# Another stated order of five engines, and a stated place for every ring tile, in a one-core attention and two-MLP kernel

## The chip, the cores and the metric

One of the cores of a Trainium2 chip runs the whole program. Five engines work side by side: TensorE (PE in the rows, with its weight loads as PEld), VectorE (DVE), ScalarE (ACT), GpSimd (POOL) and SyncE (SP), which issues all the DMAs here. The metric is the device time of one execution in microseconds; the time before is the median of 3 runs.

## The reference, cut to what matters

Causal attention with a memory term, then two MLPs, all over 2304 tokens (4 batches of 576) in float32:

```python
scores = scale * q @ k.T                       # B=4, H=8, S=576, D=64, causal
a = softmax(scores); local = a @ v
q_p = where(q > 0, q, exp(q) - 1) + 1
mem_out = (q_p @ M_prev) / (q_p . z_prev + 1e-6)
x = g * mem_out + (1 - g) * local              # g = sigmoid(beta) of each head; x is 2304 x 512
h = x @ w_in;  r = max(h, 0)                   # 512 -> 2048
x = (s * r * r + b) @ w_out                    # 2048 -> 512
h = x @ w2_in                                  # 512 -> 1024
solu = h * softmax(h)
ln = (solu - mean) / sqrt(var + 1e-6) * g_ln
out = ln @ w2_out                              # 1024 -> 512
```

## The kernel before

**Stages.** Three stages overlap at their edges. The first (to about 270 us) is the attention: 16 units (a unit u is two heads of one batch), each in five steps. `scores` multiplies K and Q (L592, and L623 for the last 64 rows), VectorE subtracts the maximum (L608, L626), ScalarE takes the exponential (L575), TensorE transposes (L649), ScalarE copies out of PSUM (L653), `values` multiplies by V (L681) and `memory` adds the memory term (L693, L697, L699). Into the gaps go the weights' decoding (L370 to L406) and the first quarter of the first MLP (`first_part`, L712 to L779). The second stage (270 to 545 us) is the rest of the first MLP: `hidden` (L712 to L720) and `ystep` (L927 to L929), over five blocks of up to 512 tokens, twice. The third (545 to 800 us) is the second MLP, nine pairs q of token tiles t = 2q and 2q + 1: `products` (42 wide matmuls, L1001 to L1004, by a scheme with seven products), `front` (softmax and layer norm), `back` (8 transpositions L1050, 24 wide matmuls L1059 to L1061, the copy L1063, the output's DMA L1064). A float32r matmul is done in three (high by high, high by low, low by high).

**Two paths that the prediction follows.** From unit 4 on, the reciprocals of a unit are turned over (L522, `turn`), copied (L524), written to DRAM (L526, tile rd) and read back, spread over the partitions (L529, tile RW, two DMAs); GpSimd multiplies phi(q) by them (L547, `weigh_q`, tile mq), and TensorE can then do L697 and L699. In the third stage the last product of a token tile is reduced on VectorE (L1007), exponentiated (L1029, ScalarE), scaled (L1030 to L1032, VectorE), squared (L1036, ScalarE), brought to a variance (L1037, VectorE), to the power -0.5 (L1038, GpSimd) and normed (L1039, VectorE); then L1050 transposes it.

**What sets the order.** The program is traced in the order of the Python code; `ORDER` then lists for every engine the numbers of its traced instructions (`606` is the 607th matmul, `71+2` stands for 71 and 72), and `state_order` chains each to the one before it, so each engine runs its list in order and waits at the first whose operands aren't there. `SLOTS` says for some rings which buffer each successive tile takes; `Slots.tile` turns the place into a tag of its own. Numbers used below: PE 606 is L522 of unit 6, 666 and 667 are its L697; PE 3656 to 3661 are the last product of token tile 10, 3774 to 3781 its transpositions; PE 4058 to 4081 and 4090 to 4113 are the output matmuls of tiles 16 and 17; SP 70 is rd of unit 6, 71 and 72 its RW, 77 a load of M_prev, 80 and 86 stores of y, 87 a load of q; SP 88 is the store of batch 1's x (tile xd, 1152 KB), 100 is rd of unit 9, 101 and 102 its RW; SP 247 to 250 are the outputs of tiles 14 to 17.

Of the kernel before, what the change touches and what calls it, by code (L numbers as in the profile page):

```python
# [17 lines left out]
P = 128  # L18
# [182 lines left out]
    "pr3": "01010101010101010101010101010101",  # L201
    "sm": "0123401234012340",
    "mq": "0101010101010101",
    "gs.r": "010101010100101010101010100",
    "gs.g": "01234012340123401234012340",
    "ys.y": "01011010010010101011",
    "ps_h.h": "010101010101010",
# [31 lines left out]
def attention_mlp_kernel(  # L239
# [74 lines left out]
    FP1 = 4  # L314
# [818 lines left out]
```

## Time and profile before

| | |
|---|---|
| median of 3 runs | 803.94 us (803.6 to 804.2) |
| the profiled execution, span | 803.9 us, 13224 instructions |
| PE busy | 794.3 us (99%), 4866 matmul records |
| PEld busy | 645.3 us (80%) |
| DVE busy | 531.6 us (66%) |
| ACT busy | 542.5 us (67%) |
| POOL busy | 107.6 us (13%) |
| DMA | 83.55 MB, mean 104 GB/s |

The ends of matmuls are modelled, so the busy time of PE says when it had work in hand and not that it ran at its peak; its pace is read from the distance between the starts of successive matmuls. The granted clock is a share of full speed: 1.00 is the upper of TensorE's two levels (2.4 GHz), 0.50 the lower (1.2 GHz).

### The profile page before, as it was taken

What the parts mean: (1) busy time and instruction counts of PE and PEld (TensorE: products, weight loads), DVE (VectorE), ACT (ScalarE), POOL (GpSimd) and SP (SyncE); (2) the same over time, 40 slices, a digit from 0 to 9 for tenths busy, and PEclk for the clock granted to TensorE, in tenths of its full rate; (3) what the DMA queues carried; (4) which work ended last, traced back from release to release, by engine and by line L of the source; (5) the groups of instructions that cost most, each with busy time, mean ns of one, the idle gap of its engine ahead of it and who ended that gap; (6) DMA issues with size and microseconds to landing.
All of it is one profiled execution on the core that took longest, in us unless ns stands there. A gap on an engine that the chain in (4) does not pass through costs nothing.

```text
span 803.9 us, 13224 instructions
## 1 busy us (share of the span) xinstructions
PE 794.3 (99%) x4866; PEld 645.3 (80%) x4866; DVE 531.6 (66%) x1329; ACT 542.5 (67%) x1122; POOL 107.6 (13%) x126
## 2 busy tenths in 40 slices
PE   9999999999999999999999999999999999999998
PEld 6677776778777788888898888889888888888886
DVE  6999988978575465245755643465788566566662
ACT  7999988888787467666677567666765455444442
POOL 3121223211010000000000020010212222222000
PEclk9999999999999999999999999999999999999999
DMA  8563666555352426424333230021210000000001
GB/s 260 185 174 112 209 211 192 187 165 155 100 170 81 160 80 220 148 78 131 131 106 131 91 119 1 28 87 70 79 53 1 26 27 27 1 27 32 22 14 66
DMA packets 42005, 83.55 MB, mean 104 GB/s; under 512 B 6652, under 2 KB 17108, under 8 KB 41940
## 3 DMA queue, kind: packets, MB, share of 16 engines
q1 hardware_dynamic: 41940, 82.71, 31.6%
q8 instruction: 38, 0.62, 0.3%
q14 instruction: 27, 0.22, 0.1%
HBM read 68.43 MB, written 14.27 MB: 103 GB/s over the span
## 4 chain that ended last, share of the span: by engine, by line
PE 81%; ACT 2%; DVE 1%; issue 0%; POOL 0%; POOLq 0%; DVEq 0%; ACTq 0%
PE h L712 8%; PE h L713 8%; PE h L714 8%; PE y L929 6%; PE y L928 6%; PE y L927 6%; PE o L1061 4%; PE o L1060 4%; PE o L1059 4%; PE pp L649 3%; PE s L592 3%; PE po L681 2%; PE zt L1050 2%; PE y L774 2%; PE y L775 2%; PE y L776 2%
## 5 line engine op out<-in xcount | busy, mean ns | idle before, releaser
L712 PE MATMUL h<-xh,w 128*128 128x512 f32 (+1 forms) x320 | 118.7, 376 | 0.3 <-ACT r L715 0.3
L713 PE MATMUL h<-xl,w 128*128 128x512 f32 (+1 forms) x320 | 117.4, 371 | 0.0
L714 PE MATMUL h<-xh,w 128*128 128x512 f32 (+1 forms) x320 | 117.2, 371 | 0.0
L715 ACT ACTIVATE r<-h 128x512 f32<-128x512 f32 (+1 forms) x80 | 43.8, 550 | 88.3 <-PE h L714 81.7
L928 PE MATMUL y<-g,w 128*128 128x512 f32 (+1 forms) x240 | 85.4, 368 | 0.0
L929 PE MATMUL y<-g,w 128*128 128x512 f32 (+1 forms) x240 | 82.5, 368 | 0.0
L927 PE MATMUL y<-g,w 128*128 128x512 f32 (+1 forms) x240 | 81.9, 368 | 0.0
L720 DVE TENSOR_TENSOR g<-r,g 128x512 fp32r<-128x512 f32 (+1 forms) x60 | 39.1, 654 | 58.7 <-ACT r L719 58.6
L653 ACT ACTIVATE pt<-pp,omg 128x256 f32<-128x256 f32 (+3 forms) x128 | 62.4, 521 | 16.5 <-PE pp L649 12.7
L575 ACT ACTIVATE pr<-pr,mx 128x512 f32<-128x512 f32 (+3 forms) x128 | 70.7, 554 | 2.5 <-DVE mx L608 2.4
L712 PEld LDWEIGHTS h<-xh,w 128*128 128x128 f32 x320 | 60.1, 188 | 12.1 <-ACT r L715 1.3
L713 PEld LDWEIGHTS h<-xl,w 128*128 128x128 f32 x320 | 60.2, 188 | 10.2 <-DVE xl L742 0.3
L714 PEld LDWEIGHTS h<-xh,w 128*128 128x128 f32 x320 | 60.1, 188 | 10.1
L608 DVE CUSTOM_DVE_ANT_0 pr<-s,big 128x128 f32<-128x128 f32 (+3 forms) x128 | 58.4, 481 | 10.5 <-PE s L592 10.1
L1060 PE MATMUL o<-w,zh 128*128 128x512 f32 x144 | 56.9, 395 | 0.0
L1061 PE MATMUL o<-w,zl 128*128 128x512 f32 x144 | 56.5, 393 | 0.0
L1059 PE MATMUL o<-w,zh 128*128 128x512 f32 x144 | 56.3, 394 | 0.0
L649 PE MATMUL pp<-ident,pr 128*128 128x128 f32 x320 | 51.3, 283 | 0.3 <-DVE ph L481 0.2
L928 PEld LDWEIGHTS y<-g,w 128*128 128x128 f32 x240 | 44.8, 188 | 7.6
L929 PEld LDWEIGHTS y<-g,w 128*128 128x128 f32 x240 | 44.6, 188 | 7.6
L927 PEld LDWEIGHTS y<-g,w 128*128 128x128 f32 x240 | 44.6, 188 | 7.4
L649 PEld LDWEIGHTS pp<-ident,pr 128*128 128x128 f32 x320 | 36.9, 142 | 15.4 <-issue 2.8
(177 smaller groups left out, 1841.9 us busy)
## 6 DMA issues: line engine op xcount, KB each, us to landing
raw<-in_moe_w_in_dram SPq DMA_DIRECT2D x24, 512.0 KB, 6.0
raw<-in_moe_w_out_dram SPq DMA_DIRECT2D x24, 512.0 KB, 3.2
kq<-in_kq_dram SPq DMA_DIRECT2D x16, 608.0 KB, 4.9
xr<-xd SPq DMA_DIRECT2D x8, 1024.0 KB, 6.9
RW<-rd SPq DMA_DIRECT2D x24, 288.0 KB, 3.9
q<-in_q_dram SPq DMA_DIRECT2D x16, 320.0 KB, 4.2
v<-in_v_dram SPq DMA_DIRECT2D x16, 320.0 KB, 3.3
xd<-xb SPq DMA_DIRECT2D x4, 1152.0 KB
```

What stands on the lines that cost most here:

```text
L575: mark[0] = nc.scalar.activation(pr, pr, AF.Exp, bias=mx, scale=-1.0, accum_out=sm).ins
L649: nc.tensor.transpose(pp[:, e * n + c * P:e * n + (c + 1) * P], pr[:, c * P:(c + 1) * P], ident)
L653: nc.scalar.activation(p["pt", i // 2][:, j, 0:i + 1, i % 2, :], pp[:, e * n:(e + 1) * n].rearrange("p (c t) -> p c t", t=P), AF.Copy, sca ...
L712: nc.tensor.matmul(ps, wc[0], xh[:, c, 0:n], start=(c == 0), stop=False)
L713: nc.tensor.matmul(ps, wc[0], xl[:, c, 0:n], start=False, stop=False)
L714: nc.tensor.matmul(ps, wc[1], xh[:, c, 0:n], start=False, stop=(c == NC - 1))
L927: nc.tensor.matmul(o, wc[0], gh[:, 0:n], start=(f == fs[0]), stop=False)
L928: nc.tensor.matmul(o, wc[1], gh[:, 0:n], start=False, stop=False)
L929: nc.tensor.matmul(o, wc[0], gl[:, 0:n], start=False, stop=(f == fs[-1]))
L1059: nc.tensor.matmul(oo, zh, w[:, 0], start=(f == 0), stop=False)
L1060: nc.tensor.matmul(oo, zh, w[:, 1], start=False, stop=False)
L1061: nc.tensor.matmul(oo, zl, w[:, 0], start=False, stop=(f == NF2 - 1))
```

## The change

Nothing that is computed changes, and no instruction is added or removed. The five lists of `ORDER` are replaced: of 4114 matmuls 3699 stand at another place (by 13 places on average), of 941 ScalarE instructions 801, of 1115 VectorE instructions 991, of 205 DMAs 154; GpSimd's list also names four set-up instructions that had been left free. The list of TensorE is in smaller pieces: 2371 breaks between runs of successive numbers, 1325 before. Every ring of tiles gets stated places (`dec`, `wpA`, `wpB`, `gs`, `ps_h`, `tiny2`, `zq` and others had none, or only for their first tiles), and `Slots` makes each buffer of a ring a tag of one buffer. The rd tile in DRAM becomes two tiles in turn. The new order was searched for with VectorE's instructions of two operands and GpSimd's products taken to exclude one another.

```diff
 ORDER = {
     "PE": """
...
-545+2 555+4 592+6 636+6 515+12 559+2 574+2 721 576 722+6 577+3 561+10 644+8 598+8 728+5 606+2 571 608+3 681 611
-766+12 682 642+2 652+4 689+4 733+6 693+2 612+12 656+12 683+6 741+8 695+4 668 699+5 826+4 704+4 778 708+10 786+6
...
-3603 3627+2 3604+7 3629+2 3638+4 3611+3 3588+6 3614+12 3642+2 3637 3631 3646+2 3668 3672+4 3669+3 3648+8 3738 3662+6
-3656+6 3676+8 3739 3700+5 3684+8 3740+2 3705+2 3692+2 3732+6 3694 3707 3695 3742+2 3696 3708 3697+2 3750 3709+18
-3744+2 3699 3774 3727+5 3775+3 3746 3778+2 3747+3 3751+5 3782 3756+4 3780+2 3760+5 3806 3765+3 3783+5 3810+2 3768
...
-4022 3974+2 4023+3 3972+2 3976+4 4021 3981+5 4004+14 4026+19 4050+8 4045+5 4058+12 4082+2 4086+4 4070+4 4084+2
-4074+8 4090+24
...
+602+3 724 598+2 605 600+2 725+7 607 732 608 606 609 681 610+2 766+3 571 769+2 652+3 642 771+4 643 682 655 775+2
+689+4 733+4 693+2 612+10 656+8 622+2 664+4 683+3 777 686+3 737+2 741+8 695+5 826 668 700 703 701+2 827 778 828
+704+13 786+6 749 739+2 750+3 779 717+4 753+10 780 829 781+2 818+4 838+8 822+2 830 783+3 831+4 792+4 765 763+2 796
...
+3662 3705+2 3677 3656 3707 3655 3614 3657+4 3738 3661 3663+2 3615 3678 3616 3739 3617+2 3665 3732 3679 3619 3733
+3680 3620+3 3681 3666+2 3623+3 3682 3740 3683+4 3744 3687+3 3774+2 3690 3776 3741 3708 3777 3691 3778+3 3709 3781
...
+4027 4056 4011+2 4057 4013 4028 4014+3 4029 4017 4030+7 4082 4037 4083 4038+2 4084+2 4040+3 4086+2 4043 4088 4058
+4089 4044 4059 4045 4060+4 4046 4064 4047+2 4065 4049 4066+5 4090+5 4071+3 4095 4074 4096 4075 4097+3 4076 4100+3
+4077 4103+3 4078+2 4106+2 4080+2 4108+6
...
     "SP": """
-17+2 20+2 32 19 24 33 25 27 31 37 22+2 26 30 46 41+2 36 49 35 34 54 45 40 39 38 28 60 29 44 43 47 65 48 50 53 69 55
-58 52 56+2 79 51 61 66 62 73 75 74 76 63+2 85 95 68 59 70 87 80 77 72 71 96 67 81 98 82 90 83+2 86 78 111 103 91+2
-110 112 94 93 88 159 121 99+2 89 109 102 101 129 163 105+2 97 116 107+2 104 114+2 117 124 119 118 125+2 165 113
-127+2 131 122 132 123 134 133 130 120 135+2 139 138 137 140 142 141 144 143 145 158 157 160 169 161+2 164 166 179
-168 167 180 170 177 181 183+2 176 185 178 186 182 187+7 195+8 194 203+2 206+3 205 210 212 209 211 213+7 234 233 236
-235 238 237 240 239 241+5 247 246 249 248 250
+17+2 20 28 45 21 19 32 25 37 23+2 22 26 33 31 36 41+2 46 35 30 49 34 39 54 38 40 60 43 27 48 47 44 65 50 53 55 58
+56+2 79 66 69 61 52 62 76 64 63 85 68 75 74 73 67 59 77 95 70 87 72 71 80 98 81 96 82 86 84 90 29 83 159 78 111 103
+91 51 89 92 110 94 93 99 121 97 100 88 101+2 116 129 105 109 106 104 108 107 114 120 112+2 117 115 118+2 123 122 163
+124 126 125 127+2 130 132 131 134 133 136 135 137+3 143 140 142 141 144 165 157+2 145 160+3 179 177 164 169 166+3
+180+3 184 170 176 185 178 190 187+2 186 189 191 183 192 196 193 195 197+2 194 200 199 201+4 207 206 205 210 208+2
+212+2 211 214+6 234 233 235+6 242 241 244 243 245+2 248+2 247 250
 """,
 }
...
+    "dec.raw": "012012012012102102101201201201201201021021021021021021021021021021",
+    "dec.wa": "012341032410324102340132403241023401213040231402341043201340231043201340213042103401",
...
 class Slots:
-    def __init__(self, pool, name=""):
-        self.pool, self.name, self.turn = pool, name, {}
-
-    def tile(self, shape, dtype, tag=None, **k):
-        places = SLOTS.get(f"{self.name}{tag}")
-        if places:
+    def __init__(self, pool, name="", bufs=1):
+        self.pool, self.name, self.bufs, self.turn = pool, name, bufs, {}
+
+    def tile(self, shape, dtype, tag=None, bufs=None, **k):
+        bufs = bufs or self.bufs
+        if tag is None:
+            return self.pool.tile(shape, dtype, bufs=bufs, **k)
+        if bufs > 1:
+            places = SLOTS.get(f"{self.name}{tag}", "")
             n = self.turn[tag] = self.turn.get(tag, -1) + 1
-            k["bufs"] = 1
-            tag += "_" + (places[n] if n < len(places) else str(n % (int(max(places)) + 1)))
-        return self.pool.tile(shape, dtype, **({"tag": tag} if tag else {}), **k)
+            tag += "_" + (places[n] if n < len(places) else "0123456789abcdef"[n % bufs])
+        return self.pool.tile(shape, dtype, tag=tag, bufs=1, **k)
 
...
-            rd = dram.tile([2, NRW, P], F32, tag="rd", name=f"rd{u}", bufs=2)
+            rd = dram.tile([2, NRW, P], F32, tag=f"rd{u % 2}", name=f"rd{u}", bufs=1)
```

## Rows read from the trace of the kernel before

In a timeline a row has the start, the duration, the engine, the line, the operation, the tiles, how many instructions the row joins, and in brackets the idle time before it with what ended it.

**Rows 1.** Stretches: length, busy time of PE, PEld, DVE, ACT, POOL, granted clock, DMA, GB/s.

```profile
24.00:120.00 96.00, 95.11 (x852) 73.34 (x854) 92.11 (x293) 91.06 (x229) 21.00 (x19) 1.00 0.56 176
130.00:250.00 120.00, 119.88 (x1028) 92.85 (x1028) 95.02 (x298) 100.80 (x256) 20.64 (x20) 1.00 0.51 156
545.00:800.00 255.00, 254.94 (x1242) 210.94 (x1240) 165.20 (x361) 131.74 (x237) 43.25 (x55) 1.00 0.08 30
```

**Rows 2.** Timeline of PE: the turning and the memory product of unit 6.

```profile
112.28 0.30 PE L522 MATMUL tr<-ident,rw 128*128 128x128 f32 x1 [0.35 <-DVE rw L515]
...
124.75 0.43 PE L697 MATMUL pe<-mq,Mb 128*64 128x64 f32 x4 [1.88 <-POOL sums L600]
```

**Rows 3.** The stretch right after that wait, columns as in rows 1.

```profile
124.75:128.25 3.50, 3.50 (x25) 3.05 (x26) 2.76 (x14) 2.03 (x6) 0.00 (x0) 0.51 0.50 197
```

**Rows 4.** Timeline of SP: the issues between unit 6's rd and RW.

```profile
115.08 0.37 SPq L779 DMA_DIRECT2D yd<-yo  x1
116.24 1.25 SPq L529 DMA_DIRECT2D RW<-rd  x2
```

**Rows 5.** Timeline of POOL: unit 6's product.

```profile
122.94 1.76 POOL L547 TENSOR_TENSOR mq<-mq,RW 128x640 f32<-128x640 f32 x1 [4.05 <-PE pe L693]
```

**Rows 6.** Timelines of PE, SP and POOL: the same path of unit 7.

```profile
130.25 0.27 PE L522 MATMUL tr<-ident,rw 128*128 128x128 f32 x1
...
132.13 1.09 SPq L529 DMA_DIRECT2D RW<-rd  x2
...
137.31 1.55 POOL L547 TENSOR_TENSOR mq<-mq,RW 128x640 f32<-128x640 f32 x1
```

**Rows 7.** Timeline of PE: the memory product of unit 14.

```profile
254.41 0.34 PE L697 MATMUL pe<-mq,Mb 128*64 128x64 f32 x4 [0.46 <-POOL mq L547]
```

**Rows 8.** Timelines of SP and POOL: RW and the product of unit 12.

```profile
216.82 1.20 SPq L529 DMA_DIRECT2D RW<-rd  x2
...
222.79 1.54 POOL L547 TENSOR_TENSOR mq<-mq,RW 128x640 f32<-128x640 f32 x1 [17.95 <-DMA RW<-rd]
```

**Rows 9.** Timeline of PE: the turning and the memory product of unit 9.

```profile
165.03 0.27 PE L522 MATMUL tr<-ident,rw 128*128 128x128 f32 x1
...
177.19 0.22 PE L697 MATMUL pe<-mq,Mb 128*64 128x64 f32 x1
```

**Rows 10.** Timelines of DVE (twice) and PE: work of two operands, and a late matmul.

```profile
222.83 2.04 DVE L726 SCALAR_TENSOR_TENSOR g<-r,b_sb,g 128x512 fp32r<-128x512 f32 x1 [0.44 <-ACT g L723]
...
536.72 1.78 DVE L720 TENSOR_TENSOR g<-r,g 128x512 fp32r<-128x512 f32 x1
...
542.90 0.38 PE L712 MATMUL h<-xh,w 128*128 128x256 f32 x1 [0.34 <-ACT r L715]
```

**Rows 11.** Timeline of PE: one transposition among wide matmuls, and eight in a row.

```profile
627.02 0.27 PE L1050 MATMUL zt<-ident,z 128*128 128x128 f32 x1
627.36 0.39 PE L1060 MATMUL o<-w,zh 128*128 128x512 f32 x1
...
702.36 0.39 PE L1001 MATMUL d<-w,yh 128*128 128x512 f32 x1
702.59 1.03 PE L1050 MATMUL zt<-ident,z 128*128 128x128 f32 x8
703.70 0.40 PE L1004 MATMUL d<-w,yl 128*128 128x512 f32 x1
```

**Rows 12.** Timelines of PE and DVE: last product and last norming, tiles 8 and 16.

```profile
689.20 0.39 PE L1004 MATMUL d<-w,yl 128*128 128x512 f32 x1
...
697.78 1.22 DVE L1039 TENSOR_SCALAR z<-z,nmu,var 128x1024 f32<-128x1024 f32 x1
...
777.15 0.40 PE L1004 MATMUL d<-w,yl 128*128 128x512 f32 x1
...
784.38 0.81 DVE L1039 TENSOR_SCALAR z<-z,nmu,var 128x1024 f32<-128x1024 f32 x1
```

**Rows 13.** The stretch of one output transfer behind the last work, columns as in rows 1.

```profile
801.65:802.50 0.85, 0.00 (x0) 0.00 (x0) 0.00 (x0) 0.00 (x0) 0.00 (x0) 1.00 0.83 308
```

More of the change, by code (lines that the diff above doesn't have):

```diff
@@ L195 @@
     "mx": ("012340123401324101420314232043104234203410324113024031024123401231024230421312410341241324103241"
-           "3021324014034213402314020421340421302412032432101421034103202103"),
+          "3021324014034213402314020421340421302412032432101421034103202103"),
     "pr1": "01010101010101010101010101010101",
@@ L202 @@
     "sm": "0123401234012340",
+    "dec.raw": "012012012012102102101201201201201201021021021021021021021021021021",
+    "dec.wa": "012341032410324102340132403241023401213040231402341043201340231043201340213042103401",
+    "wpA.w": "0123456789abcd012345678ac9bd",
     "mq": "0101010101010101",
-    "gs.r": "010101010100101010101010100",
-    "gs.g": "01234012340123401234012340",
+    "xp.xb": "01010",
+    "rt": "010101010101",
+    "gs.r": "01010101010010101010101010010101010101010101010101010101010101010101010101010101",
+    "gs.g": "01234012340123401234012340123401234012340123401234012340123401234012340123401234",
     "ys.y": "01011010010010101011",
-    "ps_h.h": "010101010101010",
+    "ps_h.h": "01010101010101010101010101010101010101010101010101010101010101010101",
+    "wpB.w": "0123456789abcd04213568ac79",
+    "tiny2.mx": "012345672103564701236457210354671023",
+    "tiny2.sm": "012301230123012301",
+    "tiny2.mu": "012301230123012301",
+    "tiny2.nmu": "012301230123012301",
+    "tiny2.var": "012301230123012301",
+    "ps_o2.o2": "010101010101010101",
+    "ps_t2.zt": "010101010101010101010101010101010101",
+    "zq.zh": "012012012012102120120120120101201201",
+    "zq.zl": "012012012012102120121021021012012012",
 }
 class Slots:
-    def __init__(self, pool, name=""):
-        self.pool, self.name, self.turn = pool, name, {}
-    def tile(self, shape, dtype, tag=None, **k):
-        places = SLOTS.get(f"{self.name}{tag}")
-        if places:
+    def __init__(self, pool, name="", bufs=1):
[6 more added lines that the diff above has]
+            places = SLOTS.get(f"{self.name}{tag}", "")
             n = self.turn[tag] = self.turn.get(tag, -1) + 1
-            k["bufs"] = 1
-            tag += "_" + (places[n] if n < len(places) else str(n % (int(max(places)) + 1)))
-        return self.pool.tile(shape, dtype, **({"tag": tag} if tag else {}), **k)
+            tag += "_" + (places[n] if n < len(places) else "0123456789abcdef"[n % bufs])
+        return self.pool.tile(shape, dtype, tag=tag, bufs=1, **k)
 def state_order(tc):
@@ L318, in attention_mlp_kernel @@
     assert 2 * FP2 <= RA + RB
-    wpA = ctx.enter_context(tc.tile_pool(name="wpA", bufs=RA))
-    dec = ctx.enter_context(tc.tile_pool(name="dec", bufs=3))
+    wpA = Slots(ctx.enter_context(tc.tile_pool(name="wpA", bufs=1)), "wpA.", RA)
+    dec = Slots(ctx.enter_context(tc.tile_pool(name="dec", bufs=1)), "dec.", 3)
     dram = ctx.enter_context(tc.tile_pool(name="dram", bufs=1, space=bass.MemoryType.DRAM))
@@ L429, in __init__ @@
             pool = lambda name, bufs, **k: Slots(actx.enter_context(
-                tc.tile_pool(name=name, bufs=bufs, side="right", **k)))
+                tc.tile_pool(name=name, bufs=1, side="right", **k)), "", bufs)
             self.ld, self.st, self.one = pool("ld", 2), pool("st", 2), pool("one", 1)
@@ L809, in attention_mlp_kernel @@
         xs = pctx.enter_context(tc.tile_pool(name="xs", bufs=1))
-        gs = Slots(pctx.enter_context(tc.tile_pool(name="gs", bufs=FP1 + 1)), "gs.")
-        xp = fctx.enter_context(tc.tile_pool(name="xp", bufs=2))
-        ys = Slots(fctx.enter_context(tc.tile_pool(name="ys", bufs=2)), "ys.")
+        gs = Slots(pctx.enter_context(tc.tile_pool(name="gs", bufs=1)), "gs.", FP1 + 1)
+        xp = Slots(fctx.enter_context(tc.tile_pool(name="xp", bufs=1)), "xp.", 2)
+        ys = Slots(fctx.enter_context(tc.tile_pool(name="ys", bufs=1)), "ys.", 2)
         ps_m = fctx.enter_context(tc.tile_pool(name="ps_m", bufs=1, space=PSUM))
@@ L877, in attention_mlp_kernel @@
         filler.append(first_part(B, fpools))
-        wpools[1] = ctx.enter_context(tc.tile_pool(name="wpB", bufs=RB, side="right", reuse_waits="tile"))
+        wpools[1] = Slots(ctx.enter_context(tc.tile_pool(name="wpB", bufs=1, side="right", reuse_waits="tile")), "wpB.", RB)
         ps_y = pctx.enter_context(tc.tile_pool(name="ps_y", bufs=1, side="right", space=PSUM, reuse_waits="tile"))
-        ps_h = Slots(pctx.enter_context(tc.tile_pool(name="ps_h", bufs=2, side="right", space=PSUM, reuse_waits="tile")), "ps_h.")
+        ps_h = Slots(pctx.enter_context(tc.tile_pool(name="ps_h", bufs=1, side="right", space=PSUM, reuse_waits="tile")), "ps_h.", 2)
         fpools[1] = [ps_h, ps_m]
@@ L957, in mlp2 @@
     def mlp2(mctx):
-        pool = lambda name, bufs, **k: mctx.enter_context(tc.tile_pool(name=name, bufs=bufs, reuse_waits="tile", **k))
+        pool = lambda name, bufs, **k: Slots(mctx.enter_context(
+            tc.tile_pool(name=name, bufs=1, reuse_waits="tile", **k)), f"{name}.", bufs)
         yp = pool("yp", 1)
```

308 rows, old and new, of the table ORDER are left out of this document.

## The prediction

> **What bounds the kernel now.** Read first the page's busy times: PE 99% of the span, the next engine 67%. Then the table of stretches: from 545 to 800 us PE is busy 254.94 of 255 us at the full clock, from 130 to 250 us 119.88 of 120, from 24 to 120 us 95.11 of 96 [rows 1]. The same instructions are run after the change, so their work stays; only idle time of PE, its clock and the spacing of neighbours can move. Third, the timeline of PE for the waits that are left: 1.88 us ahead of L697 of unit 6 [rows 2], followed by 3.5 us at the lower level of the clock, 0.51 [rows 3]; 0.46 us ahead of L697 of unit 14, with no loss of clock that the stretches show [rows 7]; 0.34 us near 543 us [rows 10]. With 0.89 us from 24 to 120, 0.12 and 0.06 us [rows 1] this makes 3.75 us of waiting inside, and 1.7 us for the clock (3.5 x 0.49). Start-up and tail come on top. So not much over 5 us is there to be won, and a search that spreads work differently can lose as much.
>
> **Unit 6, the largest gain.** L522 starts at 112.28, and PE runs out of other work 1.88 us before 124.75, at 122.87 [rows 2]: its cover is 10.6 us. GpSimd's product ends at 124.70 [rows 5], 12.4 us after L522. Part of that is SP's queue: between rd and RW it issues a load of q, a store of y (115.08) and a load of M_prev, and RW comes at 116.24 [rows 4]. The new list has rd, the load of q, RW, and the store after it; the load of M_prev comes ahead of rd. RW is then issued 1.2 us earlier, at 115.0 (the load of q stays in the way: it waits for a VectorE reduction that follows L524 in both lists). From the issue of RW to the end of the product it was 8.46 us here, with 640 KB of q, y and M_prev ahead [rows 4, 5]; 6.73 us in unit 7, with 256 KB of y ahead [rows 6]; 7.51 us in unit 12, with 576 KB ahead [rows 8]. With 320 KB ahead I take 6.9 us, nearest to unit 7: the end is 121.9, or 123.5 if the 8.46 us stays. The new list of PE moves four small products and transpositions and one wide matmul out from between L522 and L697, 0.7 to 0.8 us by their spacing in the trace, so the cover ends at 122.1. The wait left is 0 to 1.4 us. I take 0.2: a gain of 1.7. Where it is that short the clock stays up, as behind the 0.46 us of unit 14 [rows 7]: another 1.7. If the wait is 1.4, next to the 1.88 that cost the clock, both gains shrink to 0.5 together; that is the upper end.
>
> **The other units.** The pattern repeats in units 4 to 15. In unit 14 the store of y between rd and RW gives way to a load of v, and the cover grows by 0.7 us: its 0.46 us go; I take -0.4 (0 to -0.5). In unit 7 two stores and a small load come between; its product ended 8.6 us after L522 [rows 6], and by the new list PE has 11.7 us of work there (matmuls between L522 and L697 by their spacing), so 1 to 2 us more are hidden. Units 11 and 12 get a load of 608 KB in that place, no more than unit 12's 576 KB, whose product cost PE no wait [rows 8]; counted in the same way their covers are 9.6 and 11.3 us. Taken as nothing, up to 0.5 in unit 11. Unit 9 is the doubtful one: the new list puts the store of batch 1's x (SP 88, 1152 KB) between its rd and its RW. Its cover was 12.2 us from L522 to L697 [rows 9]; the list takes a tenth of it out, which leaves 10.9. RW is issued 1.9 us after L522, as in unit 7. Behind 1152 KB the rest takes 8.9 us if I go on from unit 7 to unit 12 (0.78 us for 320 KB more), or 10.8 if I go on from unit 7 to unit 6 (1.73 us for 384 KB more) [rows 4 to 6, 8]. The product is ready 10.8 to 12.7 us after L522: a wait of 0 to 1.8. I take +0.6, nearer to unit 12, whose wait the trace puts down to the transfer alone. The 0.89 us from 24 to 120 us can go, or come back double: ±0.9, taken as nothing.
>
> **VectorE and GpSimd.** The exclusion that the search assumed is visible: L726 took 2.04 us, 0.04 us after GpSimd had begun a product of 1.54 us [rows 8, 10], and L720 took 1.78 us where GpSimd's L394 ran beside it [rows 10]. Others like them stand in the trace. But where L726 stood still, the whole stretch of 120 us shows 0.12 us of PE idle [rows 1]: the time was not on the path. Behind L720 PE waited 0.34 us [rows 10]: -0.3. The lists fix the order within an engine, not the distance between engines, so some may meet again: 0 is the other end. The Trainium skill (page "SBUF — State Buffer", section "Who interferes with whom") has the rule: a VectorE instruction with two inputs in SBUF and a GpSimd instruction that reads SBUF exclude one another, and the second fully blocks. The trace agrees on the mechanism; that it pays for removing it is the third rival.
>
> **Third stage: transpositions in smaller pieces.** The old list has L1050 in 64 runs between wide matmuls, the new one in 151. A wide matmul takes 0.227 us from its start to the next (0.23 in the rows). Eight transpositions and the one wide matmul behind them take 1.11 us, to 703.70, so 0.110 each; one by itself takes 0.34 with its wide neighbour, to 627.36, so 0.113 [rows 11]. 87 more breaks cost between nothing and 1.3 us (0.015 each, the scatter of such starts); I take +0.5. The skill says otherwise (page "TensorE: Matmul & The Clock Gate", section "Step-by-step: what each phase is for"): weight loads are pulled ahead, and the next tile's load runs beside this tile's matmul. By that a lone transposition would cost its 128 columns, a quarter of a wide matmul; the row says half. It is the last rival.
>
> **Third stage: the layer norm's cover.** From the last product of a token tile to the end of L1039 it takes 8.04 us at tile 16 and 9.8 us at tile 8 [rows 12]. The old list covers it with 48 to 59 wide matmuls, so nobody waits. The new one leaves 33 (tile 10: PE 3774, the first transposition, now follows a shorter run behind 3661), 34 with a transposition (tile 8), 35 (tiles 0 and 4), 31 with eight transpositions (tile 2), and 37, 37 and 38 (tiles 12, 14, 6). At 0.227 us each, with the last product itself, that is 7.7 us for tile 10 and 8.1 to 8.8 us for the others. At the fastest chain seen only tile 10 waits, 0.3 us. The slower chains of before held other VectorE work that nobody was waiting behind, so they need not stay; between 8.04 and 8.3 us, five tiles lose 0.3 to 1.1 together: +0.8 (0 to 4).
>
> **Tail and start.** SP now issues the output of tile 14 (247) behind that of tile 16, both near the end, and tile 16's matmuls now stop six wide matmuls, 1.4 us, before the last one. A transfer of 256 KB takes 0.85 us at the end [rows 13]: +0.3 (0 to 0.85). The loads of the first 24 us change places, without one that PE's first work waits for: nothing.
>
> **The sum.** Against the profiled span of 803.9 us, which is the median of the runs (803.94): 803.9 - 1.7 - 1.7 - 0.4 - 0.3 + 0.6 + 0.5 + 0.8 + 0.3 = 802.0.
>
> **Rivals.**
> A, the cover is too short (slower). If the chain from last product to L1039 takes 9.2 us, nearer to tile 8's 9.8 than to tile 16's 8.04 [rows 12], eight tiles lose their cover's shortfall: 1.5 + 1.2 + 1.0 + 1.0 + 0.9 + 0.6 + 0.5 + 0.4 = 7.1 us in place of 0.8, and the time is 808.3. It decides from about 8.8 us on. For it: four of the new covers are below anything that the old list needed. Against: tile 16 shows that the chain runs in 8.04 when it is in a hurry.
> B, the wait moves to unit 9 (no change). Its upper end, 1.8 us, and the lower clock behind it as in unit 6 [rows 2, 3]: 802.0 - 0.6 + 1.8 + 1.7 = 804.9. Against: unit 12.
> C, all waiting inside goes. If blocked VectorE time is behind the small waits too, the 3.75 us and the 1.7 us go and only the tail is added: 803.9 - 5.4 + 0.3 = 798.8. Against it: 0.12 us of idle beside L726.
> D, transpositions among wide matmuls are half hidden: 87 x (0.113 - 0.057) = 4.9 less, and no 0.5: 796.6. Against: rows 11.
>
> **Chances.** The forecast's own case 0.55 (its range 799.8 to 804.5, from the ends of unit 6, unit 9 and the cover), A 0.17, B 0.15, C 0.11, D 0.02. A measurement of this kernel tells a change from none above about 0.2%, that is below 802.3 or above 805.5. Own case: 0.33 faster, 0.20 the same, 0.02 slower. With A slower but for 0.02, B the same but for 0.02, and C and D faster: faster 0.46, same 0.35, slower 0.19. For 8 in 10 the range takes half of C and most of A: 798.6 to 807.5.
>
> **What would show it.** PE idle ahead of L697 of unit 6 below 0.5 us, with the clock at 1.00 from 120 to 130 us; the same of unit 9 below 1 us; L1050's waits on VectorE at tiles 0 to 10 of 1 us together; a lone transposition at 0.113 us. The forecast is wrong if L1050 waits at every tile, or if a wait of over a microsecond with a fall of the clock stands anywhere else in the attention.

## The result: 0.5% slower

| | before | after |
|---|---|---|
| median of the runs | 804.07 us (803.6 to 805.43, 4 runs) | 808.25 us (807.81 to 810.54, 4 runs) |
| ratio | | 1.0054 (95%: 1.0039 to 1.0069) |
| span of the profiled execution | 803.9 us | 806.5 us |
| PE busy | 794.3 us | 793.8 us |

The forecast was 802.0, and 808.25 lies outside its range. The time of an execution is not its span: the profiled execution of after took 808.23 us for a span of 806.5, and every execution for which both are listed has 1.7 to 1.9 us around its span. The profiled execution of before, at 803.9, must then have taken about 805.7 (an estimate from these distances), some 1.6 us more than the median of before. Between ordinary executions the difference is therefore 4 us, not the 2.6 us of the two spans.

The stretches after (length, busy time of PE, PEld, DVE, ACT, POOL, granted clock, DMA, GB/s; compare rows 1):

```profile
24.00:120.00 96.00, 95.38 (x838) 70.35 (x838) 93.70 (x292) 93.29 (x235) 21.32 (x18) 1.00 0.55 174
120.00:130.00 10.00, 9.38 (x104) 7.01 (x100) 9.63 (x33) 8.61 (x24) 3.22 (x5) 1.00 0.56 189
130.00:250.00 120.00, 117.93 (x1025) 89.49 (x1027) 91.60 (x294) 98.94 (x247) 19.26 (x18) 1.00 0.54 161
250.00:270.00 20.00, 20.00 (x158) 14.79 (x155) 7.72 (x24) 9.52 (x21) 3.10 (x2) 1.00 0.29 93
270.00:530.00 260.00, 258.60 (x1250) 217.59 (x1249) 141.66 (x255) 173.01 (x296) 9.34 (x7) 1.00 0.33 109
530.00:545.00 15.00, 15.00 (x82) 12.92 (x81) 5.71 (x11) 10.15 (x20) 0.00 (x0) 1.00 0.28 89
545.00:800.00 255.00, 254.19 (x1235) 208.39 (x1234) 170.16 (x361) 133.96 (x238) 41.39 (x55) 1.00 0.09 32
```

The clock is whole everywhere, units 14 and 15 and the stretch to 545 us no longer wait, and 2.07 us of idle stand where rows 1 had 0.12, 1.40 where the second stage had none, 0.81 where the third had 0.06. The list of PE's waits after (line, what released it, sum, times, longest) names them:

```profile
PE tq L629 <- ACT RW L617: 1.7, 1, 1.7
PE y L834 <- ACT yo L838: 1.4, 1, 1.4
PE po L759 <- POOL sums L660: 1.1, 1, 1.1
PE pe L757 <- POOL sums L660: 1.0, 2, 0.6
PE zt L1111 <- DVE z L1100: 0.4, 2, 0.2
```

The lines have moved by 60 (61 in the third stage): L757 is the old L697, L759 the old L699, L1100 the old L1039, L1111 the old L1050. In the edited kernels some lists are shorter or longer by a few lines, and the lines differ again by as many: L1078 and L1111 below are the same transposition.

### The profile page after: what moved, and what is told of

Read it like the earlier page. It is cut to its first block, busy times and chain, and to the rows that moved or that the text cites. A ratio compares the mean times of both kernels' runs of the same rounds, so it can differ in the third digit from the quotient of the medians.

```text
span 806.5 us, 13270 instructions
## 1 busy us (share of the span) xinstructions
PE 793.8 (98%) x4866; PEld 638.1 (79%) x4866; DVE 536.0 (66%) x1329; ACT 545.3 (68%) x1122; POOL 105.1 (13%) x126
## 4 chain that ended last, share of the span: by engine, by line
PE 68%; DVE 3%; issue 3%; DMA 2%; ACT 1%; POOL 1%; SPq 0%; POOLq 0%; ACTq 0%; DVEq 0%
PE h L773 7%; PE h L774 7%; PE h L772 7%; PE y L987 6%; PE y L989 6%; PE y L988 6%; PE o L1121 3%; PE o L1122 3%; PE o L1120 3%; PE pp L709 2%; PE zt L1111 2%; PE y L834 1%; PE y L835 1%; PE y L836 1%; PE po L741 1%
## 5 line engine op out<-in xcount | busy, mean ns | idle before, releaser
L772 PE MATMUL h<-xh,w 128*128 128x512 f32 (+1 forms) x320 | 116.9, 378 | 0.0
L774 PE MATMUL h<-xh,w 128*128 128x512 f32 (+1 forms) x320 | 114.3, 374 | 0.0
L987 PE MATMUL y<-g,w 128*128 128x512 f32 (+1 forms) x240 | 82.3, 369 | 0.0
L989 PE MATMUL y<-g,w 128*128 128x512 f32 (+1 forms) x240 | 82.2, 369 | 0.0
L988 PE MATMUL y<-g,w 128*128 128x512 f32 (+1 forms) x240 | 81.0, 369 | 0.0
L635 ACT ACTIVATE pr<-pr,mx 128x128 f32<-128x128 f32 (+3 forms) x128 | 71.0, 557 | 3.8 <-DVE mx L668 3.8
L713 ACT ACTIVATE pt<-pp,omg 128x128 f32<-128x128 f32 (+3 forms) x128 | 62.3, 524 | 13.3 <-PE pp L709 10.9
L773 PEld LDWEIGHTS h<-xl,w 128*128 128x128 f32 x320 | 59.9, 188 | 10.7 <-DVE wa L436 0.6
L668 DVE CUSTOM_DVE_ANT_0 pr<-s,big 128x512 f32<-128x512 f32 (+3 forms) x128 | 58.9, 480 | 5.9 <-ACT pr L635 2.8
L709 PE MATMUL pp<-ident,pr 128*128 128x128 f32 x320 | 58.8, 278 | 0.6 <-DVE ptl L722 0.3
L778 ACT ACTIVATE g<-r,b_sb,s_sb 128x512 fp32r<-128x512 f32 (+1 forms) x60 | 45.4, 767 | 15.3 <-PE y L989 14.7
L1121 PE MATMUL o<-w,zh 128*128 128x512 f32 x144 | 54.9, 399 | 0.0
L1120 PE MATMUL o<-w,zh 128*128 128x512 f32 x144 | 54.9, 398 | 0.0
L709 PEld LDWEIGHTS pp<-ident,pr 128*128 128x128 f32 x320 | 39.2, 140 | 14.6 <-issue 2.6
L987 PEld LDWEIGHTS y<-g,w 128*128 128x128 f32 x240 | 44.7, 188 | 7.5
L989 PEld LDWEIGHTS y<-g,w 128*128 128x128 f32 x240 | 44.5, 188 | 7.4
```

The lines of the kernel that those rows point to most:

```text
L635: mark[0] = nc.scalar.activation(pr, pr, AF.Exp, bias=mx, scale=-1.0, accum_out=sm).ins
L709: nc.tensor.transpose(pp[:, e * n + c * P:e * n + (c + 1) * P], pr[:, c * P:(c + 1) * P], ident)
L713: nc.scalar.activation(p["pt", i // 2][:, j, 0:i + 1, i % 2, :], pp[:, e * n:(e + 1) * n].rearrange("p (c t) -> p c t", t=P), AF.Copy, sca ...
L772: nc.tensor.matmul(ps, wc[0], xh[:, c, 0:n], start=(c == 0), stop=False)
L773: nc.tensor.matmul(ps, wc[0], xl[:, c, 0:n], start=False, stop=False)
L774: nc.tensor.matmul(ps, wc[1], xh[:, c, 0:n], start=False, stop=(c == NC - 1))
```

## The experiments

**The base of the sum: the kernel before once more.** No edit.

> The kernel before once more, for a second profile of it. Theory: the profiled execution that the prediction was built on had a fall of TensorE's clock behind unit 6's wait that most executions don't have; of the executions timed so far some lie at 803.4 to 804.2 us and some at 806.0 to 806.2, and 1.7 to 1.8 us lie around each span. Without the fall the span is about 802.3 and the clock 1.00 from 120 to 130 us, with the wait of about 1.9 us still there; with the fall the span is about 804.2. Rival: the executions differ in something else, and the clock falls in a run of 803.9 too.

It took 804.48 us with a span of 802.7. The timelines of PE, DVE and POOL and one stretch of this execution, around unit 6:

```profile
123.38 0.34 PE L697 MATMUL pe<-mq,Mb 128*64 128x64 f32 x4
125.26 0.55 PE L649 MATMUL pp<-ident,pr 128*128 128x128 f32 x3 [1.07 <-DVE xb L701]
...
121.83 1.81 DVE L376 TENSOR_SCALAR wa<-wa 128x512 int32<-128x512 int32 x1
124.99 0.21 DVE L701 COPY xb<-pe 128x64 f32<-128x64 f32 x1
...
121.47 1.86 POOL L547 TENSOR_TENSOR mq<-mq,RW 128x640 f32<-128x640 f32 x1 [2.20 <-DMA RW<-rd]
...
124.00:128.00 4.00, 2.93 (x27) 2.11 (x26) 4.00 (x20) 3.50 (x10) 0.00 (x0) 1.00 0.72 269
```

No fall of the clock, as the theory has it. But its other half falls: the wait ahead of L697, 1.88 us in [rows 2], is 0.11 us here, and another stands behind it, 1.07 us ahead of L649 for L701. L376, a type conversion of the weight decoding that takes 0.37 to 0.43 us in its 47 other places, took 1.81: GpSimd's product had begun 0.36 us earlier. Everything behind it on VectorE came 1.4 us late. The profile that the prediction read shows none of this, because there RW was late and L376 long done.

**Unit 6's DMAs alone, on the kernel before.**

```diff
-... 59 70 87 80 77 72 71 96 ...     # SP, kernel before
+... 59 77 70 87 72 71 80 96 ...
```

> The kernel before with one part of the change alone: around unit 6, SP's load of M_prev (77) goes ahead of rd and the store of y (80) behind RW. Every other list is that of before. Theory: RW is issued 1.2 us earlier, PE's wait of 1.88 us ahead of L697 falls to 0.2 to 0.6 us, no fall of the clock follows in any execution, and the time is about 802.4 us with little scatter. Rival: the moved store holds y's buffer, or M_prev holds rd, so another wait of a microsecond appears in the same stretch and the time stays at 804.

Measured: ratio 0.9993 (0.9982 to 1.0004), 10 runs. L697 waits 0.13 us, and the 1.07 us ahead of L649 are there again. The edit on which the forecast put 3.4 us gives nothing that can be measured. The timelines of PE, SP and POOL, of this run and then of the kernel after, show why:

```profile
113.57 0.30 PE L522 MATMUL tr<-ident,rw 128*128 128x128 f32 x1 [0.36 <-DVE rw L515]
116.49 1.09 SPq L529 DMA_DIRECT2D RW<-rd  x2
122.51 1.73 POOL L547 TENSOR_TENSOR mq<-mq,RW 128x640 f32<-128x640 f32 x1 [2.33 <-DMA RW<-rd]
...
113.12 0.27 PE L582 MATMUL tr<-ident,rw 128*128 128x128 f32 x1
116.89 1.11 SPq L589 DMA_DIRECT2D RW<-rd  x2
122.47 1.55 POOL L607 TENSOR_TENSOR mq<-mq,RW 128x640 f32<-128x640 f32 x1 [3.19 <-DMA RW<-rd]
```

The edit issues RW 2.9 us after the turning (3.6 in the second profile of before, 4.0 in the first), but GpSimd's product ends 10.7 us after it, as in the second profile of before; in the first it was 12.4. The earlier issue did not bring the product earlier. In the kernel after RW is issued 3.8 us after the turning, 0.2 earlier than the profile of before has it and not the 1.2 of the forecast, and the product ends 10.9 us after it.

**The meeting of L376 and L547 taken away, on the kernel before; then both.**

```diff
-... 259 315 278 272 279+2 274 330 263 281 ...     # DVE, kernel before; 315 is L376, 263 L701
+... 259 278 272 279+2 274 330 263 315 281 ...
```

> The kernel before with one VectorE instruction moved: the type conversion L376 of the weight decoding that runs at 122.8 us goes behind L701 of unit 6, three places of this list's work later. In the second profile of the kernel before, and with unit 6's DMAs mended, it took 1.81 us in place of 0.41, because GpSimd's product L547 began 0.25 us earlier; all behind it was 1.4 us late, L701 among it, and PE waited 1.07 us ahead of L649 for L701. Theory: what binds behind unit 6 in ordinary executions is this meeting; with it gone PE's wait ahead of L649 falls to 0.3 us or less, the span is about 801.5 and the time 1.0 us under the kernel before. Rival: the conversion meets something else at its new place or holds up the decoded weights, or the wait for RW (0.1 to 1.9 us, by the execution) takes its place; then the time stays within 0.4 us of before.

> The kernel before with both parts at unit 6: the two DMAs of SP as in e5_u6 and the one VectorE instruction as in e9_dve1. Theory: each alone leaves the other's wait; with both, PE waits less than 0.5 us between 120 and 130 us in every execution, and the time is 1.2 us under the kernel before, with less scatter than it has. Rival: 0.5 us or more of waiting comes back in the same stretch.

Timelines of PE and DVE with both parts:

```profile
122.84 0.34 PE L697 MATMUL pe<-mq,Mb 128*64 128x64 f32 x4 [0.24 <-POOL sums L600]
...
123.27 0.21 DVE L701 COPY xb<-pe 128x64 f32<-128x64 f32 x1
123.40 0.41 DVE L376 TENSOR_SCALAR wa<-wa 128x512 int32<-128x512 int32 x1
```

L376 takes 0.41 us again, L649 doesn't wait, and the profiled execution has the shortest span of all, 800.9 us. So the mechanism is as the theory says. Its size shows in the profiles: from L522 of unit 6 to L522 of unit 7 it is 15.97 us in the second profile of before and in the one with the DMAs alone, 15.09 here. The times are too coarse for it: 0.9992 (0.9983 to 1.0000) and 0.9991 (0.9980 to 1.0002) hold the gains that were expected, 1.0 and 1.2 us, and next to none as well. In the profiled execution of the first, unit 5 waited 1.80 us for RW and the clock fell behind it; the ten executions of the second lie between 802.7 and 806.9 us. Neither is shown to beat the kernel before.

**The start.** After, ScalarE waits for weights and PE behind it (timelines of ACT and PE, kernel after):

```profile
19.83 0.66 ACT L435 ACTIVATE wa<-raw 128x512 f32<-128x512 f32 x1 [2.19 <-DMA raw<-in_moe_w_in_dram]
20.39 0.58 ACT L617 ACTIVATE RW<-tr 128x512 f32<-128x512 f32 x1
...
21.02 0.33 PE L629 MATMUL tq<-ident,ph 128*128 128x128 f32 x1 [1.69 <-ACT RW L617]
```

```diff
-17+2 20 28 45 21 19 32 25 37 23+2 22 26 33 31 36 ...     # SP, kernel after
+17+2 20 28 45 21 19 32+2 25 37 23+2 22 26 31 36 ...      # first edit
+17+2 20+2 32 19 24 33 25 27 31 37 22 28 45 23 26 36 ...  # second edit
```

> The changed kernel with one DMA moved back: the second load of first-layer weights (SP 33) is issued right behind the first (SP 32), as before the change, and no longer behind two loads of M_prev and two of v. Theory: the 2.19 us in which ScalarE waits for these weights at 17.6 us hold up RW and so PE's 1.69 us ahead of L629 at 21 us; that wait falls under 0.4 us and the span goes from 806.5 to about 805.2. Rival: the queue of the first 20 us is full whatever the order, so the wait moves to the work that needs v or M_prev (L741 or L759, 1 us or more) and the span stays within 0.4 us of 806.5.

> The changed kernel with the first 13 DMAs of SP in the order of before (the small loads b and M_prev of batch 1 behind them), the rest as changed. Theory: the start lost 1.7 us at L629 because small loads and M_prev took the place of weights, K, Q and V that the first two units need; with all of them back, and not one alone, PE's waits from 12 to 24 us are under 0.9 us together and the span is about 805.2. Rival: the other engines' new order needs M_prev or b that early; then a wait of over 1 us appears at L759 or on ScalarE and PE loses it again.

With one load moved the rival is right: the weights are there at 17.5 us, and the load of v that they displaced is late (PE, first edit):

```profile
18.41 0.96 PE L741 MATMUL po<-pt,v 128*64 128x256 f32 x8 [2.23 <-DMA v<-in_v_dram]
```

The span is 809.9. With the first 13 loads as before the waits from 12 to 24 us are gone, but the span is 806.0, not 805.2, because unit 6 takes the gain (PE, second edit), where after had 0.61:

```profile
124.33 0.34 PE L757 MATMUL pe<-mq,Mb 128*64 128x64 f32 x4 [1.62 <-POOL sums L660]
```

**Unit 7's second half of RW.**

```diff
-... 86 84 90 29 83 159 ...     # SP, kernel after
+... 86 84 83 90 29 159 ...
```

> The changed kernel with the second half of unit 7's RW (SP 83) issued right behind its first half (SP 84), no longer behind a store of y and the load of gl. Theory: PE's 1.10 us ahead of L759 at 141.9 us is that half coming late; it falls to 0.2 us or less, and the span goes from 806.5 to about 805.5. Rival: the wait comes from the traffic of the loads around it, not from the place in the list; then it stays above 0.7 us.

L759 no longer waits, here and in the three other runs with this edit; some 0.50 us ahead of the next turning come in its place in all four. The span is 804.3, 2.2 less, more than this wait.

**The store of y.** After, the load of x (xr) is issued ahead of a store of y (timelines of SP, ACT and PE):

```profile
293.56 0.56 SPq L856 DMA_DIRECT2D xr<-xd  x1
296.16 0.33 SPq L839 DMA_DIRECT2D yd<-yo  x1
...
302.56 0.39 ACT L838 ACTIVATE yo<-y 128x256 f32<-128x256 f32 x1 [1.64 <-DMA yd<-yo]
...
303.00 0.39 PE L834 MATMUL y<-g,w 128*128 128x256 f32 x1 [1.40 <-ACT yo L838]
```

```diff
-... 160+3 179 177 164 169 166+3 180 ...     # SP, kernel after
+... 160+3 179 164 169 166+3 177 180 ...
```

> The changed kernel with the 1024 KB load of the next block's x (SP 177) moved behind the store of y SP 168, as before the change. Theory: the store of y at 296.2 us takes 6.3 us to land because this load is ahead of it; its buffer comes free late, ScalarE's copy L838 waits 1.64 us for it and PE 1.40 us ahead of L834. With the load behind, PE's wait goes to 0.1 us or less and the span to about 805.1. Rival: the buffers of y are too few for the new order of the matmuls; then 0.8 us or more of the wait stay.

The wait is gone, here and in the run of five places below. In seven other runs that leave this load ahead of the store it is there, 0.47 to 2.01 us long. So the 1 MB ahead of the store is its cause, and its length differs from execution to execution. Half of the 1.40 comes back where that x is used (PE):

```profile
408.85 0.39 PE L987 MATMUL y<-g,w 128*128 128x256 f32 x1 [0.69 <-DVE yT L1012]
```

The span is 805.6, with a fall of the clock at 22 us in it.

**Five places of SP's list at once.** The three edits (the first of the start), and

```diff
-... 117 115 118+2 123 ... 245+2 248+2 247 250     # SP, kernel after
+... 117 118+2 115 123 ... 245+6
```

> The changed kernel with five places of SP's list mended at once: the three of the other runs, unit 11's load of kq (SP 115) moved behind its RW, and the output of token tile 14 (SP 247) issued ahead of that of tile 16. All other engines keep the new order. Theory: what the change lost in the first two stages and the tail was lost in SP's order: 1.4 + 1.0 + 1.4 + 0.4 + 0.3 us come back, the span is about 802.0 and the time about 803.7, even with the kernel before. Rival: the time that comes back is lost again at the next wait; then the span stays above 804.

Ratio 1.0080 (1.0060 to 1.0100), no better than the change as it is (1.0054); the two intervals overlap. The rival is right: the late load of kq (115) makes PE wait 1.73 us for it at 201 us, the load of v at the start 1.58, the late x 1.14 at 408.

**The third stage's transpositions put together.** Each goes to the place of the last of its four:

```diff
-... 3744 3687+3 3774+2 3690 3776 3741 3708 3777 3691 3778+3 3709 3781 ...     # PE, kernel after
+... 3744 3687+3 3690 3741 3708 3774+4 3691 3709 3778+4 ...
```

> The changed kernel with the third stage's transpositions L1111 put together: each is moved to the place of the last of its four, so that 77 runs become 34; nothing else moves. Theory: a break costs 0.012 us (a lone transposition takes 0.124 us in the trace, one of a run 0.111), so the third stage gains 0.5 us, and the waits ahead of L1111 stay as they are, 0.8 us; the span is about 806.0. Rival: a break costs the 0.04 us that the whole stage's pace has lost by (1.05 us over 25 breaks more than before the change); then 1.7 us come back and the span is about 804.8.

The span, 809.4, is that of an execution with a long wait at unit 6 and a fall of the clock at the start. The stage itself is told by the distances between starts: with 0.2275 us for a wide matmul and 0.1105 for a transposition, the blocks with transpositions last 3.05 us longer than that in the kernel after, 0.57 in the kernel before, and 1.18 here, with one new wait of 0.59 for yl. Most of what came back are waits: gathered, the first transposition of a tile comes later.

The blocks are not the whole stage. PE's last matmul of the second stage and its last of all, before and then after:

```profile
602.41 0.39 PE L929 MATMUL y<-g,w 128*128 128x512 f32 x1
799.79 0.39 PE L1061 MATMUL o<-w,zl 128*128 128x512 f32 x1
...
603.79 0.39 PE L989 MATMUL y<-g,w 128*128 128x512 f32 x1
802.05 0.39 PE L1122 MATMUL o<-w,zl 128*128 128x512 f32 x1
```

They lie 197.38 us apart before (197.4 in the second profile too) and 198.26 after, with four wide matmuls (0.91 us) fewer between them: the third stage costs 1.8 us more, not the 2.48 of the blocks, because the wide matmuls outside them kept the pace better after (0.26 us over it in all, 0.95 before). Gathering the transpositions makes the stage 0.7 us shorter than in the kernel after.

**Behind the old first two stages.** The lists of before for stages one and two, those of the change for the third.

> The kernel before in its first two stages, with the third stage's instructions of all five engines in the order of the change (its stated places for zq, tiny2 and dec.wa too). Theory: the new third stage costs about 2 us by itself: L1050 (L1111 of the change) waits at eight tiles for a total of 2.0 to 2.5 us by the distance of starts, and the tail adds 0.3; the span is 2.0 to 2.5 us over that of an ordinary execution of the kernel before (802.5 on average), about 804.7, and the ratio of times about 1.0027. Rival: the waits of the third stage come from how late the second stage of the change leaves VectorE and GpSimd; behind the old second stage they are under 0.7 us, and the ratio is within 1.000 +- 0.001.

The time, 1.0234 (1.0195 to 1.0272), can't be used: where the two orders are joined, one load of kq comes 7.8 us late and the third stage starts with waits of 3.3 and 1.0 us. From 690 us on the stage runs undisturbed, and there the waits are those of the change (PE here; then PE after):

```profile
693.27 0.30 PE L1078 MATMUL zt<-ident,z 128*128 128x128 f32 x1 [0.19 <-DVE var L1065]
714.05 0.41 PE L1078 MATMUL zt<-ident,z 128*128 128x128 f32 x2 [0.23 <-DVE z L1067]
```

```profile
676.20 0.30 PE L1111 MATMUL zt<-ident,z 128*128 128x128 f32 x1 [0.19 <-DVE var L1098]
696.98 0.41 PE L1111 MATMUL zt<-ident,z 128*128 128x128 f32 x2 [0.23 <-DVE z L1100]
```

These waits belong to the third stage's own lists.

**GpSimd's products beside the last step of the layer norm.** L1100 has one full-size operand (z); nmu and var are single columns. After, it takes 1.21 to 1.23 us at nine tiles of 18, 0.95 at one, and 0.81 where no product starts just ahead of it; before, 1.22 at three [rows 12, tile 8], none of which PE waited for. One such place after (PE, DVE, POOL):

```profile
696.37 0.39 PE L1120 MATMUL o<-w,zh 128*128 128x512 f32 x1
...
695.62 1.22 DVE L1100 TENSOR_SCALAR z<-z,nmu,var 128x1024 f32<-128x1024 f32 x1
...
695.55 0.74 POOL L1041 TENSOR_TENSOR s<-yT 128x256 f32<-128x256 f32 x1
```

From the start of L1120 at 696.37 to that of L1111 at 696.98 are 0.61 us, 0.38 over the pace, while the row speaks of 0.23 idle: the modelled end of a wide matmul lies 0.16 us past the start of the next one, so a wait behind a wide matmul is 0.16 longer than it reads.

```diff
-... 81 86 76 84 77 85 82 ... 95 110 100 108 101 109 106 ...       # Pool, kernel after
+... 81 76 86 77 84 85 82 ... 95 100 110 101 108 109 106 ...       # first edit
+... 81 76+2 86 84+2 82 ... 95 100+2 110 108+2 106 ...             # second edit
```

> The changed kernel with four instructions of GpSimd moved one place forward: where a product L1041 follows directly on the power L1099 of the layer norm, in four of the six tiles whose transpositions wait visibly (at about 614, 616, 696 and 701 us of the profile after), L1041 goes ahead of L1099. Nothing else moves. Theory: the norming L1100, a VectorE instruction with one tile as operand, takes 1.22 us where a GpSimd product starts just before it, and 0.81 elsewhere; it was not counted among the work that excludes GpSimd. With L1041 ahead, the four L1100 take 0.81 us, the waits ahead of L1111 behind them (0.31, 0.29, 0.44 and 0.35 us by the distance of starts) fall under 0.1 each, the other two (0.39 and 0.29) stay, and the third stage is 1.2 us shorter. Rival: the chain from the last product to L1100 is too long by itself; then L1100 takes 0.81 and the waits stay within 0.1 us of what they were, or GpSimd's product now delays L1099 by as much.

> The changed kernel with four products of GpSimd moved forward by two or three places, so that at two of the six waiting tiles (at about 614 and 696 us of the profile after) no product follows on the power L1099 any more; in e12_pool the next product had moved up into the place of the one taken away, so that L1100 took 1.22 us as before. At the other four tiles the products stay. Theory: at these two tiles L1100 takes 0.81 us in place of 1.22 and the wait ahead of L1111 falls from 0.31 and 0.44 us (distance of starts) to 0.1 or less; at the other four L1100 stays at 0.95 to 1.22 and the waits at 0.29 to 0.39. Rival: the chain is too long by itself; then the waits of the two tiles stay as well, though L1100 is shorter, because something ahead of it is late, or L1099 comes 0.4 us later behind the products.

The first edit failed at what it set out to do: the next product moved up beside L1100, and nothing changed (ratio 1.0048, 1.0032 to 1.0063). The second, at a tile that was freed and at one that was not (DVE and PE):

```profile
696.07 0.81 DVE L1100 TENSOR_SCALAR z<-z,nmu,var 128x1024 f32<-128x1024 f32 x1
701.26 1.22 DVE L1100 TENSOR_SCALAR z<-z,nmu,var 128x1024 f32<-128x1024 f32 x1
...
697.07 0.38 PE L1111 MATMUL zt<-ident,z 128*128 128x128 f32 x2
702.63 0.41 PE L1111 MATMUL zt<-ident,z 128*128 128x128 f32 x2 [0.17 <-DVE z L1100]
```

At both freed tiles L1100 takes 0.81 us and the wait is gone; at the others both stay. So at these two tiles the wait came from the product beside L1100; for the other tiles with a long L1100 and a wait that is inferred. The stage as a whole became 0.9 us longer: waits of PE appear further on, which read 0.24 us at 627 us and 0.70 at 706. That the products, put earlier, hold other work there is a reading that no run tested.

**The mended versions.** First: SP's start as before, unit 6's load of q behind RW, unit 7's RW, the load of x one place later, the tail, the transpositions. Second: unit 7's RW, the tail and the transpositions alone.

> The changed kernel with the places mended that the runs so far showed to cost: SP's first 13 DMAs as before; unit 6's load of q (87) behind its RW; the second half of unit 7's RW (83) right behind the first; the load of x (177) one place later, behind the store of y 164; the output of token tile 14 ahead of that of tile 16; and the third stage's transpositions in 34 runs. The other engines' lists are those of the change. Theory: 1.3 us of the start, 0.6 at unit 6, 2.0 behind unit 7, 1.1 at the store of y, 0.7 in the third stage and 0.3 in the tail add up, since the wait in which the start's gain was lost (unit 6) is mended too: the span is about 800.5 and the time 802.3, 0.2% under the kernel before. Rival: the DMA queue only hands the waits on, as with single places mended; then the span stays above 803.

> The changed kernel with three places mended: unit 7's second half of RW right behind the first, the output of token tile 14 ahead of that of tile 16, and the third stage's transpositions in 34 runs. Theory: 2.0 us behind unit 7 (0.5 at unit 7 itself, the rest in units 8 to 11, where SP comes earlier), 0.7 in the third stage and 0.3 in the tail come back, the span is about 803.5 and the time about 805.3. Rival: the 2.0 us were the scatter of one execution; then the time is about 807.

The first is at 1.0054 (1.0040 to 1.0067). The load of q behind RW was the mistake (DVE and PE):

```profile
121.99 1.34 DVE L538 TENSOR_SCALAR ph<-q 128x640 f32<-128x640 f32 x1 [3.43 <-DMA q<-in_q_dram]
...
124.67 0.69 PE L750 MATMUL pe<-ptl,v 128*64 128x64 f32 x16 [3.29 <-ACT pt L710]
```

The second is at 1.0039 (1.0018 to 1.0061), with executions from 806.1 to 813.2: not the 805.3 expected, and its interval overlaps that of the change. That the 2.2 us at unit 7 came from the edit is not borne out; the rival, the scatter of one execution, forecast about 807 and fits better.

## Why the prediction was wrong, step by step

| step | forecast, us | shown, us |
|---|---|---|
| unit 6's wait | -1.7 | -0.6: 0.11 + 1.07 in the second profile of before, 0.61 after |
| the clock behind it | -1.7 | 0: not in an ordinary execution of before (a fall there costs 1.2) |
| unit 14 | -0.4 | -0.5 |
| VectorE and GpSimd near 543 us | -0.3 | -0.3 |
| unit 9 behind the store of x | +0.6 | 0 |
| unit 11 | 0 | +0.4 |
| unit 7's second RW | 0 | +1.1 |
| the start | 0 | +0.9 (PE busy from 10 to 24 us: 13.07 before, 12.12 after) |
| store of y in the second stage | not seen | +1.4 |
| transpositions in pieces | +0.5 | +0.2 at most |
| the layer norm's cover | +0.8 | +1.8: the whole third stage, pieces included (2.48 in its blocks) |
| tail | +0.3 | +0.3 (4.02 us from PE's end to the span's, 3.70 before) |

They sum to +4.5, the pieces being part of the cover's row; two waits of 0.47 us of the second profile of before (at 24 and 140 us) that after doesn't have make it 3.6, and the two spans differ by 806.5 - 802.7 = 3.8. Waits under 0.3 us are left out, so the sum closes only to a few tenths of a microsecond.

*The base.* The sum was made against 803.9 "which is the median of the runs". That was a span set equal to a time. The profiled execution was one with a fall of the clock, and 1.7 us of the forecast's gain were the return of something the median never paid.

*Unit 6.* The step that failed is "a gain of 1.7": it took the wait that ended last in one execution for the bound. Behind it stood another wait, hidden there, on VectorE. The change does away with most of both (0.61 us are left), but what they cost in the second profile of before is 1.2 us. Two terms beneath the gain failed as well. "RW is then issued 1.2 us earlier" came to 0.2 us, and with the DMAs alone an RW 0.7 us earlier than in the second profile left the product where it was. The 8.46 us from issue to product, which the forecast put down to the 640 KB ahead, were 7.1 in the second profile with the same list.

*Waits that the lists add.* The start was dismissed with "without one that PE's first work waits for". ScalarE's third piece of weights was such a load, not for itself but for RW queued behind it. Unit 7 was dismissed by its first half of RW; L759 needs the second, which the list put behind a store and another load. The load of x ahead of the stores of y was not looked for, since only the path from rd to RW was followed through SP's list.

*The cover.* Rival A's mechanism, at a quarter of its size (1.8 of 7.1 us): from last product to L1100 the even tiles take 7.4 to 9.0 us from start to end, where the forecast allowed 8.04 to 8.3. That A's time, 808.3, is the measured 808.25 is luck: no even tile's chain takes A's 9.2 us, and the rest of the loss stands at places that A doesn't name. The forecast's covers were counted rightly, but the old list's 48 to 59 wide matmuls leave out tile 16, which had 38. The missing term is the meeting of L1100 with GpSimd's products, shown at two tiles. The prediction said that blocked VectorE time "was not on the path", read from a stage where the covers were long; with the covers cut to 33 to 38 wide matmuls it was. The change's search kept VectorE's work of two operands away from GpSimd's products. L376 and L1100 have one full-size operand and were held all the same: 1.81 us against 0.41, and 1.22 against 0.81. The Trainium skill (page "SBUF — State Buffer", section "Who interferes with whom") names tensor_scalar among the instructions that can take the shared pair of ports, when its operands allow; the traces agree, and the prediction quoted from that section the rule on two inputs only.

*The pieces.* The count in the prediction was wrong: L1050 stands in 52 runs before and 77 after, not 64 and 151. Outside the waits the blocks with transpositions take 0.41 us over the pace before (0.57 less one wait of 0.16) and 3.05 - 2.46 = 0.59 after (eight blocks with 0.15 to 0.44 us make the 2.46): 25 breaks cost 0.2 us at most. That they are not half hidden either, against rival D, stands: the stage became 1.8 us longer.

Right were unit 14, the wait near 543 us and the tail. Unit 9's wait is 0.04 us, the low end of its 0 to 1.8.

Open are the single prices of the start, unit 7 and the store of y. Each mended place moved the next wait, and executions differ by up to 5 us, so only the wait itself is shown for them. Where its list is left as the change has it, the wait at the start reads 1.59 to 1.86 us over the profiles, that of L759 0.43 to 1.24, and that of L757 of unit 6 0.21 to 2.33: the sizes in the table are those of one execution. Whether TensorE waits less with the whole list of SP exchanged was not tried; the old list of one engine and the new ones of the others wait for each other.

## What to carry to other kernels

Take two profiles before you price a wait: if it has another length in the second, the price is that of the next wait behind it, and a fall of the clock in one of them is no gain to be had. Compare times with times; the distance between an execution's time and its span has to be known before a sum is made against either. Where an order shortens a cover, list everything that can hold the chain beneath it, instructions with one full-size operand beside GpSimd's included, and follow every moved DMA to the buffer that it frees as well as to the data that it brings.

## What the runs showed of the hardware

The clock fell in some executions behind a wait of PE, and whether it falls can't be read from the wait's length. It fell behind 1.59, 1.78, 1.82, 1.86 and 2.23 us at the start, 1.80 at unit 5 and 1.88 at unit 6; it did not behind 1.59, 1.69 and 1.73 at the start, nor behind 2.33 and 3.29 at unit 6. The profiled execution of before, with its one fall, has a mean clock of 0.998. A mean of 0.998 or less stands in 5 of the 69 other executions of that kernel, in none of the 4 of the change, and in 5 of the 10 of the run with the first edit of GpSimd's list, whose first two stages are those of the change.

What a fall costs is less than the 1.7 us that the forecast took for it. L522 of units 6 and 7 lie 17.97 us apart in the profile of before [rows 2, 6] and 15.09 in the run with both parts (PE):

```profile
112.00 0.30 PE L522 MATMUL tr<-ident,rw 128*128 128x128 f32 x1 [0.36 <-DVE rw L515]
...
127.09 0.27 PE L522 MATMUL tr<-ident,rw 128*128 128x128 f32 x1
```

Of the 2.88 us between them 1.64 are the longer wait of L697 (1.88 against 0.24), which leaves 1.2 for the clock. At the start it is 1.5: with the load of x moved the clock falls behind L629, which starts at 21.02 us as in the kernel after, and L709, at 52.03 us after, comes at 53.52. One stretch each of the runs with the load of x and with the first edit of the start moved:

```profile
23.00:25.00 2.00, 2.00 (x12) 1.36 (x9) 0.75 (x3) 1.24 (x4) 0.00 (x0) 0.50 0.01 4
```

```profile
18.40:22.00 3.60, 3.59 (x23) 2.86 (x25) 0.66 (x2) 1.16 (x2) 0.00 (x0) 0.59 0.22 90
```

Executions of one and the same program on one core scatter: the kernel before took 803.15 to 808.23 us over the groups of runs used here, with medians from 804.07 to 805.49; in the profiles of it and of its edits it is the landing of RW, in units 5 and 6, that differs most.
